# Moving loads, casts and transposes in the hand-ordered prologue of a fused linear-attention and MLP kernel

## The chip, the cores and the metric

The kernel runs on one core of one Trainium2 chip. The metric is the device time of one execution in microseconds (us). The time before is 209.86 us, the median of 5 runs that lie between 209.24 and 211.7.

The core's engines are named as the profile names them: PE is TensorE (matrix products and transposes through the PE array, results in PSUM), DVE is VectorE, ACT is ScalarE, POOL is GpSimd, SP is SyncE, which here only issues DMAs. In the timeline each engine works through its own list in order, and waits for other engines through semaphores.

## What is computed

```python
B, H, S, D = 4, 8, 768, 64                       # q, k, v: [B, H, S, D] float32
for b in range(S // 64):                         # blocks of 64 positions
    intra = (qb @ kb.T) * Dmask                  # Dmask[i, j] = lam_h ** (i - j) for i >= j
    out   = intra @ vb + (qb * lam_pow) @ state  # state: D x D per batch and head
    state = lam ** 64 * state + (kb * rev_pow).T @ vb
x  = out.transpose(0, 2, 1, 3).reshape(B, S, 512)
xn = (x - mean) / sqrt(var + 1e-6) * g_ln
y  = x + relu(xn @ w_ch1) @ w_ch2                # w_ch1: 512 x 2048 (W1), w_ch2: 2048 x 512 (W2)
```

## The kernel before

**Tiling.** The 3072 tokens are cut into 12 windows of 256 positions, numbered u = 0 to 11; window u belongs to batch u mod 4 and to part u div 4 of its sequence. So windows 0 to 3 are the first parts of the four batches. (The change's name calls a window a pair, of two 128-token tiles: the second pair is u = 1, the third u = 2, the fourth u = 3.) A window's k, q and v are three loads of 512 KB each (window 0 in halves of 256 KB). W1 and W2 lie in four pieces each, cast to 16 bits on the way in; the trace counts a piece as 512 KB of what is written.

**Attention of a window.** `in_k` and `in_k_one` cast k to bf16 (L215, L231). `in_q` and `in_q_one` scale q by powers of lam (L226 by halves of the heads, HA and HB; L236 by position parity, all heads). `in_v` scales v (L242). For windows 0 to 2 `transpose_pe` turns k and q on PE into a PSUM tile `tp`, which ACT, or DVE if so told, copies into `kqT` (L250, L251); from window 3 on `transpose_dma` has SP issue a DMA transpose instead (L257). `scores` makes the products of q and k for two of the four head pairs (L273) and `mask` masks them on DVE (L283). `kv` makes the new state's products (L307) and `new_state` the decayed sum (L313, L317, L332). `av` applies the masked scores to v (L419) and `inter` adds the state's part (L432). `inter(u, 0)` ends with `reader(u)`, a DVE copy of eight columns called `seen` (L443): the later `inter(u, 1)` writes the same PSUM tile `po`, so on PE it waits for `seen`. `norm` takes mean and variance and makes the centred tile `xc` (for u >= 2 ACT sums at L458 and DVE makes `xc` at L460); `to_xT` transposes `xc` (L493) and ACT copies it (L494) to `xT`.

**MLP of a window.** A `unit` of the first product is 8 matmuls of 128x256 (L530) and one ACT relu (L533). For windows 0 and 1, `m1a.tile`/`m1b.tile` do the first W1 piece one 128-token tile at a time with 16 matmuls (L641, relu L644). `m1s(m1a, c, lo, hi)` takes the units of W1 piece c. The second product of windows 0 and 1 goes in four parts of 4 matmuls per tile (L667), part n with W2 piece n. DVE finishes a tile at L691.

**Order.** `tc.manual_schedule()` leaves every engine's order as written. Only semaphores for data and for the reuse of buffers are added. From L942 on the calls are listed by hand; `units(n)` interleaves the next n steps of the MLP's list `plan` (L1016 to L1025: first the units of `m1b`, then parts 0 to 3 of the second product).

**Loads.** SP issues the loads of k, q and v (L76), POOL those of W1 (L117) and W2 (L120), since they cast. There are three gates. `behind(t)` is a tiny POOL copy (L728) that waits for the load of `t`, and so holds POOL's later instructions back. `open_in(u, True)` writes one element of the k buffer with a POOL memset (L91), which SP's load of that k, and SP's queue behind it, waits for. And a load that POOL issues after a cast on POOL can't be issued before that cast's own input has landed. POOL's order in the prologue before is: `behind` k of window 0, W1 piece 0, k cast of window 0's HB, v of window 0, `behind` k of window 1, W1 pieces 1 and 2, q of window 1, W1 piece 3, W2 piece 0, v of window 1, `behind` W1 piece 2, memset for window 2, `behind` W2 piece 0, W2 pieces 1 and 2, q of window 2, W2 piece 3, v of window 2, memset for window 3.

Of the kernel before, what the change touches and what calls it, by code (L numbers as in the profile page):

```python
# [12 lines left out]
ACT = mybir.ActivationFunctionType  # L13
# [4 lines left out]
def kernel(  # L18
# [97 lines left out]
    def load_w1(c):  # L116
        nc.gpsimd.dma_start(w1[c], moe_w_ch1[:, c * W1C:(c + 1) * W1C].rearrange("(k p) f -> p k f", p=128))  # L117

    def load_w2(c):
        nc.gpsimd.dma_start(w2[c], moe_w_ch2[c * W2K * 128:(c + 1) * W2K * 128, :].rearrange("(k p) d -> p k d", p=128))  # L120
# [90 lines left out]
    def in_k(u, eng, hs=ALL):  # L211
        src = qkv_in[u]["k"][:, hs].rearrange("p (a e) j d -> p a e j d", e=2)
        dst = part(0, st[u]["kq"], hs)
        for j in range(2):
            (eng.copy if eng is nc.scalar else eng.tensor_copy)(dst[:, :, :, j], src[:, :, :, j])  # L215
# [17 lines left out]
    def in_q_one(u, eng, j):  # L233
        src = qkv_in[u]["q"].rearrange("p (a e) j d -> p a e j d", e=2)
        lq = (lam_q[:, :, j] if u < LB else lam_p[:, 0, :]).rearrange("p (a e) -> p a e", e=2)
        eng.tensor_tensor(part(1, st[u]["kq"], ALL)[:, :, :, j], src[:, :, :, j],  # L236
                          lq[:, :, :, None].to_broadcast([128, NP, 2, D]), op=ALU.mult)

    def in_v(u, eng, hs=ALL):
        n = hs.stop - hs.start  # L240
        lv = lam_v[:, hs, :, None] if u < LB else lam_p[:, 1, hs, None, None]
        eng.tensor_tensor(st[u]["vb"][:, hs], qkv_in[u]["v"][:, hs], lv.to_broadcast([128, n, 2, D]), op=ALU.mult)  # L242

    def transpose_pe(u, a, pairs, eng=None):
        s = st[u]
        n = len(pairs)
        tp = mm_tile([128, n, 2, 128], BF16, "tp")
        for i, p in enumerate(pairs):
            for j in range(2):
                nc.tensor.transpose(tp[:, i, j, :], s["kq"][:, a, p, j], ident)  # L250
        (eng.tensor_copy if eng else nc.scalar.copy)(s["kqT"][:, a, pairs[0]:pairs[0] + n], tp)  # L251
# [27 lines left out]
    def mask(u, hf, heads=(0, 1)):  # L279
        s = st[u]  # L280
        kp = keep.rearrange("p a b t -> p a (b t)")
        for e in heads:
            nc.vector.tensor_tensor(s[f"mA{hf}"][:, e], s[f"sc{hf}"][e],  # L283
                                    kp[:, None, :, :].to_broadcast([128, 2, 2, 128]), op=ALU.mult)
# [30 lines left out]
    def state_sum(u, ab):  # L315
        tmp = wk.tile([128, NP, D], F32, tag="Stmp", name="Stmp")
        nc.vector.tensor_tensor(tmp, st[u]["pk"][ab], state[u % B], op=ALU.add)  # L317
        return tmp
# [154 lines left out]
    def keep_x(u, copy):  # L473
        for ab in range(2):
            copy(st[u]["x"][:, ab], st[u]["po"][ab].rearrange("p h d -> p (h d)"))

    def to_xT(u, ab):
        s = st[u]
        t = 2 * u + ab
        g = group_of[t]  # L480
        i = t - groups[g][0]
        if i == 0:
            xT_of[g] = gp.tile([128, KA, GT * 128], BF16, tag="xT", bufs=3, name="xT")
        dst = xT_of[g][:, :, i * 128:(i + 1) * 128]
        if u >= 2 and u not in X_PE:
            nc.sync.dma_start_transpose(dst, s["xc"][:, ab])
        else:
            if u < 2:
                xt = mm_tile([128, KA, 128], BF16, "xt")
            else:  # L490
                xt = ps.tile([128, KA, 128], BF16, tag=f"po{ab}", name="xt")
            for kk in range(KA):
                nc.tensor.transpose(xt[:, kk, :], s["xc"][:, ab, kk * 128:(kk + 1) * 128], ident)  # L493
            nc.scalar.copy(dst, xt)  # L494
# [230 lines left out]
    def behind(tile_ap):  # L725

        seen_p = wk.tile([128, 1], F32, tag="seen_p", name="seen_p")
        nc.gpsimd.tensor_copy(seen_p, tile_ap)  # L728
# [21 lines left out]
    for i in range(2):  # L750
        nc.scalar.activation(lam_p[:, i], lnlam, ACT.Exp, scale=e_p[:, i:i + 1])
    in_q(0, nc.vector, HA)
    behind(qkv_in[0]["k"][:, 0, 0, 0:1])
    load_w1(0)
    in_k(0, nc.gpsimd, HB)
    in_q(0, nc.vector, HB)
    transpose_pe(0, 1, (0, 1))
    transpose_pe(0, 0, (2, 3), nc.vector)
# [184 lines left out]
    in_k(1, nc.scalar)  # L943
    norm(0, 0, early=True)
    reader(0)
    behind(qkv_in[1]["k"][:, 0, 0, 0:1])
    load_w1(1)
    load_w1(2)
    in_q_one(1, nc.gpsimd, 0)
    in_q_one(1, nc.gpsimd, 1)  # L950
    load_w1(3)
    load_w2(0)
    in_v(1, nc.gpsimd)
    behind(w1[2][:, 0, 0:1])
    open_in(2, True)
    load_in(2, "k", nc.sync)
    load_in(2, "q", nc.sync)
    load_in(2, "v", nc.sync)
    transpose_pe(1, 0, (0, 1), nc.vector)
    transpose_pe(1, 0, (2, 3), nc.vector)  # L960
    to_xT(0, 0)
    inter(0, 1)
    norm(0, 1, early=True)
    st[0]["tmp"] = state_sum(0, 1)
    m1a.tile(0, 0)
    to_xT(0, 1)
    transpose_pe(1, 1, (0, 1), nc.vector)
    transpose_pe(1, 1, (2, 3))
    m1a.tile(0, 1)
    keep_x(0, nc.vector.tensor_copy)  # L970
    nc.scalar.activation(sqrt_first, eps_t, ACT.Sqrt)
    scores(1, 0)
    scores(1, 1, early=True)
    mask(1, 0)
    mask(1, 1)
    m1s(m1a, 1, 0, 1)
    kv(1, "sc")
    new_state(1, 0, nc.scalar)
    m1s(m1a, 1, 1, 2)
    rstd_of(0)  # L980
    m1s(m1a, 2, 0, 1)
    av(1, (0, 1))
    av(1, (2, 3))
    inter(1, 0)
    norm(1, 0, early=True)
    m1s(m1a, 2, 1, 2)
    inter(1, 1)
    norm(1, 1, early=True)
    st[1]["tmp"] = state_sum(1, 1)
    m1s(m1a, 3, 0, 1)  # L990
    to_xT(1, 0)
    m1s(m1a, 3, 1, 2)
    to_xT(1, 1)
    open_window(2)
    in_k_one(2, nc.vector, 0)
    in_k_one(2, nc.vector, 1)
    m1b.tile(0, 0)
    m1b.tile(0, 1)
    keep_x(1, nc.scalar.copy)
    rstd_of(1)  # L1000
    behind(w2[0][:, 0, 0:1])
    load_w2(1)
    load_w2(2)
    in_q_one(2, nc.gpsimd, 0)
    in_q_one(2, nc.gpsimd, 1)
    load_w2(3)
    in_v(2, nc.gpsimd)
    open_in(3, True)
    load_in(3, "k", nc.sync)
    load_in(3, "q", nc.sync)  # L1010
    load_in(3, "v", nc.sync)
    open_in(4, False)
    load_in(4, "k", nc.sync)
    load_in(4, "q", nc.sync)
    load_in(4, "v", nc.sync)
    plan = [(m1b, n) for n in range(m1b.count // NWC, m1b.count)]  # L1016
    plan += [(m2, i, part) for part in range(KB // 4) for m2, i in ((m2a, 0), (m2a, 1), (m2b, 0))]
    plan += [(m2b, 1, part) for part in range(KB // 4)]
# [10 lines left out]
    def units(n):  # L1029
        for _ in range(n):  # L1030
            f, *a = next(steps)
            f(*a)


    units(1)
    transpose_pe(2, 0, (0, 1, 2, 3))
    units(2)
    transpose_pe(2, 1, (0, 1, 2, 3))
    new_state(0, 1, nc.gpsimd)
    new_state(1, 1, nc.gpsimd)  # L1040
# [1 line left out]
    s1b(2)  # L1042
    units(2)
    s2(2)
    units(2)
    s0(2)
    units(2)
    s3(2)
    units(2)
    s4(2)  # L1050
    open_window(3)
    in_k_one(3, nc.vector, 0)
    in_k_one(3, nc.vector, 1)
# [2 lines left out]
    in_v(3, nc.gpsimd)  # L1056
    transpose_dma(3, 0)
    transpose_dma(3, 1)
    units(2)
    open_in(5, False)  # L1060
    load_in(5, "k", nc.sync)
# [296 lines left out]
```

## Time and profile before

| what | value |
|---|---|
| median of 5 runs | 209.86 us (209.24 to 211.7) |
| the profiled execution's own time | 210.09 us |
| its span, first to last instruction | 208.4 us |
| PE busy in the span | 197.4 us, 95% |
| PE work after 200 us (the tail) | 4.39 us of 8.40 us |

The span is the profiled execution between its first and last instruction; what lies around it is 210.09 - 208.4 = 1.7 us. In a timeline row the first number is the start and the second the length, in us from the span's start; then come engine, line, operation, what it writes and reads, shapes and count, and in brackets the engine's idle time just before and what ended it. Where rows of one kind follow each other they are merged into one.

When each load of the prologue was issued (timeline) and when it landed (issue plus the time to landing of the DMA view):

| load | issued | to landing | landed |
|---|---|---|---|
| k, window 1 | 5.43 | 6.7 | 12.1 |
| W1 piece 0 | 5.70 | 8.8 | 14.5 |
| q, window 1 | 6.22 | 9.6 | 15.8 |
| v, window 1 | 7.97 | not told | |
| W1 piece 1 | 12.32 | 8.3 | 20.6 |
| W1 piece 2 | 13.13 | 10.1 | 23.2 |
| W1 piece 3 | 17.87 | 7.9 | 25.7 |
| W2 piece 0 | 18.67 | 10.0 | 28.7 |
| k, window 2 | 23.55 | 6.5 | 30.1 |
| q, window 2 | 23.96 | 8.1 | 32.1 |
| v, window 2 | 24.59 | 9.0 | 33.6 |
| W2 piece 1 | 29.27 | 7.8 | 37.1 |
| W2 piece 2 | 30.07 | 11.0 | 41.1 |
| W2 piece 3 | 34.14 | 10.4 | 44.5 |
| k, window 3 | 36.95 | 8.7 | 45.6 |
| q, window 3 | 37.41 | 9.7 | 47.1 |
| k, window 5 | 54.38 | 4.7 | 59.1 |

### The profile page before, as it was taken

What the parts mean: (1) busy time and instruction counts of PE and PEld (TensorE: products, weight loads), DVE (VectorE), ACT (ScalarE), POOL (GpSimd) and SP (SyncE); (2) the same over time, 40 slices, a digit from 0 to 9 for tenths busy, and PEclk for the clock granted to TensorE, in tenths of its full rate; (3) what the DMA queues carried; (4) which work ended last, traced back from release to release, by engine and by line L of the source; (5) the groups of instructions that cost most, each with busy time, mean ns of one, the idle gap of its engine ahead of it and who ended that gap; (6) DMA issues with size and microseconds to landing.
All of it is one profiled execution on the core that took longest, in us unless ns stands there. A gap on an engine that the chain in (4) does not pass through costs nothing.

```text
span 208.4 us, 7231 instructions
## 1 busy us (share of the span) xinstructions
PE 197.4 (95%) x3099; PEld 156.2 (75%) x3099; DVE 137.0 (66%) x277; ACT 120.0 (58%) x277; POOL 84.0 (40%) x116
## 2 busy tenths in 40 slices
PE   1988999999999999999999999999999999999992
PEld 0477787554775577478888888888888888888881
DVE  2588570529584877758798775667776857865253
ACT  3865779235245567448566775485596575652630
POOL 4649138319847340627255440871282202002020
PEclk9999999999999999999999999999999999999999
DMA  4999999999999999994897899898968020078403
GB/s 108 298 271 216 209 298 164 192 273 273 186 319 175 218 166 217 210 255 83 182 211 111 181 213 159 204 199 121 227 134 190 6 50 3 16 129 278 139 5 97
DMA packets 91043, 36.39 MB, mean 175 GB/s; under 512 B 65154, under 2 KB 88194, under 8 KB 91011
## 3 DMA queue, kind: packets, MB, share of 16 engines
q1 hardware_dynamic: 86400, 31.53, 72.2%
q0 software_dynamic: 4224, 4.19, 12.7%
q8 instruction: 24, 0.39, 0.8%
q10 hardware_dynamic: 386, 0.20, 0.4%
q14 instruction: 9, 0.07, 0.2%
HBM read 27.27 MB, written 6.29 MB: 161 GB/s over the span
## 4 chain that ended last, share of the span: by engine, by line
PE 76%; DMA 12%; DVE 5%; SPq 2%; POOL 2%; issue 1%; POOLq 0%; ACT 0%; DVEq 0%
PE pm L530 33%; PE pm L667 14%; PE pwd L565 6%; PE pwa L565 6%; PE pwc L565 6%; DMA w<-in_moe_w_ch_dram 5%; DMA qin<-in_q_dram 4%; DMA kin<-in_k_dram 3%; PE pwb L565 3%; SPq L76 2%; PE po L432 1%; PE po L419 1%; DVE x L578 1%; PE sc L273 1%; DVE wt L788 1%; PE po L406 1%
## 5 line engine op out<-in xcount | busy, mean ns | idle before, releaser
L530 PE MATMUL pm<-xT,w 128*128 128x256 bf16 x736 | 84.9, 273 | 0.4 <-DMA w<-in_moe_w_ch_dram 0.3
L530 PEld LDWEIGHTS <-w 128*128 128x128 bf16 x736 | 70.4, 98 | 10.2 <-DMA w<-in_moe_w_ch_dram 0.8
L533 ACT ACTIVATE hT<-pm 128x512 f16<-128x512 f32 x92 | 53.9, 597 | 30.1 <-PE pm L530 30.0
L667 PE MATMUL pm<-w,hT 128*128 128x512 f16 x128 | 30.2, 380 | 0.0
L565 PEld LDWEIGHTS <-hs 128*128 128x128 f16 x256 | 24.9, 98 | 2.9
L590 POOL TENSOR_TENSOR x<-ev_u,x 128x256 f32<-128x256 f32 x8 | 5.8, 725 | 51.3 <-ACT ev_u L589 39.9
L313 POOL TENSOR_TENSOR Sn<-Stmp,lam_s 128x256 bf16<-128x256 f32 x16 | 9.8, 615 | 37.9 <-DVE Stmp L391 18.4
L548 DVE TENSOR_TENSOR hs<-hT 128x1024 f16<-128x1024 f16 x16 | 13.9, 872 | 16.0 <-ACT hT L533 15.9
L667 PEld LDWEIGHTS <-hT 128*128 128x128 f16 x128 | 11.6, 98 | 12.1
L565 PEld LDWEIGHTS <-hT 128*128 128x128 f16 x192 | 18.8, 98 | 2.2
L283 DVE TENSOR_TENSOR mA<-sc,keep 128x512 bf16<-128x512 f32 x20 | 13.1, 683 | 7.1 <-PE sc L273 7.1
L458 ACT ACTIVATE x<-po 128x512 f32<-128x512 f32 x18 | 10.6, 590 | 9.9 <-PE po L419 5.3
L460 DVE SCALAR_TENSOR_TENSOR xc<-po,nmean,g_row 128x512 bf16<-128x512 f32 x18 | 13.0, 746 | 3.7 <-ACT nmean L459 3.6
L236 POOL TENSOR_TENSOR kq<-qin,lam_q 128x512 bf16<-128x512 f32 x10 | 10.4, 1063 | 7.5 <-DMA qin<-in_q_dram 7.5
L503 ACT ACTIVATE sq<-x,nmean 128x512 bf16<-128x512 f32 x18 | 12.9, 719 | 0.3
L242 POOL TENSOR_TENSOR vb<-vin,lam_p 128x1024 bf16<-128x1024 f32 x6 | 11.4, 1896 | 3.0 <-DMA vin<-in_v_dram 2.9
L242 POOL TENSOR_TENSOR vb<-vin,lam_v 128x1024 bf16<-128x1024 f32 (+1 forms) x7 | 11.8, 1688 | 1.1 <-ACT kqT L251 0.9
L494 ACT COPY xT<-xt 128x512 bf16<-128x512 bf16 x10 | 5.8, 582 | 7.7 <-PE xt L493 7.7
L578 DVE SCALAR_TENSOR_TENSOR x<-pwd,rstd,x 128x256 f32<-128x256 f32 x16 | 7.7, 482 | 3.6 <-POOL x L598 3.6
L236 POOL TENSOR_TENSOR kq<-qin,lam_p 128x512 bf16<-128x512 f32 x9 | 9.3, 1042 | 1.9 <-DMA qin<-in_q_dram 1.9
L578 DVE SCALAR_TENSOR_TENSOR x<-pwa,rstd,x 128x512 f32<-128x512 f32 (+1 forms) x16 | 9.1, 612 | 0.8
L565 PE MATMUL pwa<-w,hT 128*128 128x256 f16 x64 | 9.6, 273 | 0.0
(129 smaller groups left out, 298.6 us busy)
## 6 DMA issues: line engine op xcount, KB each, us to landing
out_dram<-x SPq DMA_DIRECT2D x22, 256.0 KB, 3.8
w<-in_moe_w_ch_dram POOLq DMA_DIRECT2D x8, 512.0 KB, 9.4
kin<-in_k_dram SPq DMA_DIRECT2D x14, 256.0 KB, 5.1
qin<-in_q_dram SPq DMA_DIRECT2D x14, 256.0 KB, 4.6
vin<-in_v_dram SPq DMA_DIRECT2D x14, 256.0 KB, 5.1
kin<-in_k_dram SPq DMA_DIRECT2D x5, 512.0 KB, 6.7
qin<-in_q_dram SPq DMA_DIRECT2D x5, 512.0 KB, 8.8
vin<-in_v_dram SPq DMA_DIRECT2D x5, 512.0 KB, 8.4
```

What stands on the lines that cost most here:

```text
L236: eng.tensor_tensor(part(1, st[u]["kq"], ALL)[:, :, :, j], src[:, :, :, j], lq[:, :, :, None].to_broadcast([128, NP, 2, D]), op=ALU.mult)
L242: eng.tensor_tensor(st[u]["vb"][:, hs], qkv_in[u]["v"][:, hs], lv.to_broadcast([128, n, 2, D]), op=ALU.mult)
L283: nc.vector.tensor_tensor(s[f"mA{hf}"][:, e], s[f"sc{hf}"][e], kp[:, None, :, :].to_broadcast([128, 2, 2, 128]), op=ALU.mult)
L458: nc.scalar.activation(x, po, ACT.Copy, accum_out=sm)
L460: nc.vector.scalar_tensor_tensor(xc, in0=po, scalar=nm, in1=g_row, op0=ALU.add, op1=ALU.mult)
L503: nc.scalar.activation(sq, s["x"][:, ab], ACT.Square, bias=s["nmean"][:, ab:ab + 1], accum_out=ss[:, ab:ab + 1])
L530: nc.tensor.matmul(pm[:, b, :], lhsT=w1[n // W2K][:, kk, (n % W2K) * 128:(n % W2K + 1) * 128], rhs=xT_of[g][:, kk, 0:N], start=(b == 0 and ...
L533: nc.scalar.activation(hT[:, u * NB:(u + 1) * NB, 0:N], pm, ACT.Relu)
L548: nc.vector.tensor_tensor(s13, b[:, :, 1:2, :].to_broadcast([128, n, 2, 128]), b[:, :, 0:4:3, :], op=ALU.subtract)
L565: nc.tensor.matmul(pr[bank], lhsT=lhs(r), rhs=rhs, start=(first and r == 0), stop=(r == KB // 2 - 1), skip_group_check=True)
L578: nc.vector.scalar_tensor_tensor(out, in0=in0, scalar=r[ab], in1=in1, op0=ALU.mult, op1=ALU.add)
L667: nc.tensor.matmul(acc[i], lhsT=hT[:, kk, i * 128:(i + 1) * 128], rhs=w2[kk // W2K][:, kk % W2K, :], start=(kk == 0), stop=(kk == KB - 1))
```

## The change

The work is the same: the same matmuls, casts and loads. What moves:

- W1 piece 0 is issued by POOL after the cast of window 0's second half of k, no longer ahead of it behind the landing of the first half. W1 pieces 1, 2 and 3 are each issued behind a cast of window 1: q's HA, q's HB, v.
- W2 pieces 0 and 1 are issued behind the landing of window 2's k, pieces 2 and 3 behind window 2's q casts.
- On PE, window 1's first two q transposes come ahead of the first `m1a` tile, and its scores ahead of the second; the copy of those transposes goes from DVE to ACT, and so does `keep_x(0)`. The table load for the square root, `rstd_of(0)` and `rstd_of(1)` move to after window 2's scores.
- Window 3's casts and DMA transposes move from after window 2's second `inter` and norm to before window 2's `av`. On SP the load of window 4's v comes after those transposes.

```diff
     in_q(0, nc.vector, HA)
-    behind(qkv_in[0]["k"][:, 0, 0, 0:1])
+    in_k(0, nc.gpsimd, HB)
     load_w1(0)
-    in_k(0, nc.gpsimd, HB)
     in_q(0, nc.vector, HB)
...
     reader(0)
-    behind(qkv_in[1]["k"][:, 0, 0, 0:1])
+    in_q(1, nc.gpsimd, HA)
     load_w1(1)
+    in_q(1, nc.gpsimd, HB)
     load_w1(2)
-    in_q_one(1, nc.gpsimd, 0)
-    in_q_one(1, nc.gpsimd, 1)
+    in_v(1, nc.gpsimd)
     load_w1(3)
-    load_w2(0)
-    in_v(1, nc.gpsimd)
     behind(w1[2][:, 0, 0:1])
     open_in(2, True)
     load_in(2, "k", nc.sync)
     load_in(2, "q", nc.sync)
     load_in(2, "v", nc.sync)
+    behind(qkv_in[2]["k"][:, 0, 0, 0:1])
+    load_w2(0)
+    load_w2(1)
     transpose_pe(1, 0, (0, 1), nc.vector)
     transpose_pe(1, 0, (2, 3), nc.vector)
     to_xT(0, 0)
     inter(0, 1)
     norm(0, 1, early=True)
     st[0]["tmp"] = state_sum(0, 1)
+    transpose_pe(1, 1, (0, 1))
     m1a.tile(0, 0)
+    transpose_pe(1, 1, (2, 3))
     to_xT(0, 1)
-    transpose_pe(1, 1, (0, 1), nc.vector)
-    transpose_pe(1, 1, (2, 3))
+    scores(1, 0)
+    mask(1, 0)
+    scores(1, 1, early=True)
+    mask(1, 1)
+    keep_x(0, nc.scalar.copy)
     m1a.tile(0, 1)
-    keep_x(0, nc.vector.tensor_copy)
-    nc.scalar.activation(sqrt_first, eps_t, ACT.Sqrt)
-    scores(1, 0)
-    scores(1, 1, early=True)
-    mask(1, 0)
-    mask(1, 1)
-    m1s(m1a, 1, 0, 1)
     kv(1, "sc")
     new_state(1, 0, nc.scalar)
-    m1s(m1a, 1, 1, 2)
-    rstd_of(0)
-    m1s(m1a, 2, 0, 1)
+    m1s(m1a, 1, 0, 2)
     av(1, (0, 1))
     av(1, (2, 3))
     inter(1, 0)
     norm(1, 0, early=True)
-    m1s(m1a, 2, 1, 2)
+    m1s(m1a, 2, 0, 1)
     inter(1, 1)
     norm(1, 1, early=True)
     st[1]["tmp"] = state_sum(1, 1)
+    m1s(m1a, 2, 1, 2)
+    to_xT(1, 0)
     m1s(m1a, 3, 0, 1)
-    to_xT(1, 0)
+    to_xT(1, 1)
     m1s(m1a, 3, 1, 2)
-    to_xT(1, 1)
     open_window(2)
     in_k_one(2, nc.vector, 0)
     in_k_one(2, nc.vector, 1)
+    in_q_one(2, nc.gpsimd, 0)
+    in_q_one(2, nc.gpsimd, 1)
     m1b.tile(0, 0)
     m1b.tile(0, 1)
     keep_x(1, nc.scalar.copy)
-    rstd_of(1)
-    behind(w2[0][:, 0, 0:1])
-    load_w2(1)
     load_w2(2)
-    in_q_one(2, nc.gpsimd, 0)
-    in_q_one(2, nc.gpsimd, 1)
     load_w2(3)
+    open_in(3, True)
     in_v(2, nc.gpsimd)
-    open_in(3, True)
     load_in(3, "k", nc.sync)
     load_in(3, "q", nc.sync)
     load_in(3, "v", nc.sync)
     open_in(4, False)
     load_in(4, "k", nc.sync)
     load_in(4, "q", nc.sync)
-    load_in(4, "v", nc.sync)
...
-    units(1)
+    units(2)
     transpose_pe(2, 0, (0, 1, 2, 3))
-    units(2)
+    units(1)
     transpose_pe(2, 1, (0, 1, 2, 3))
...
     s2(2)
+    nc.scalar.activation(sqrt_first, eps_t, ACT.Sqrt)
+    rstd_of(0)
+    rstd_of(1)
     units(2)
     s0(2)
-    units(2)
-    s3(2)
-    units(2)
-    s4(2)
     open_window(3)
     in_k_one(3, nc.vector, 0)
     in_k_one(3, nc.vector, 1)
     in_q_one(3, nc.gpsimd, 0)
     in_q_one(3, nc.gpsimd, 1)
     in_v(3, nc.gpsimd)
     transpose_dma(3, 0)
     transpose_dma(3, 1)
+    load_in(4, "v", nc.sync)
+    units(2)
+    s3(2)
+    units(2)
+    s4(2)
     units(2)
```

Here `s1b(2)` and `s2(2)` are window 2's two halves of scores and mask, `s0(2)` its `kv` and states, `s3(2)` is `av(2)`, `inter(2, 0)` and the norm of its first tile, `s4(2)` is `inter(2, 1)` and the norm of its second tile.

More of the change, by code (lines that the diff above doesn't have):

```diff
@@ L1032, in units @@
             f(*a)
+    units(2)
+    transpose_pe(2, 0, (0, 1, 2, 3))
     units(1)
-    transpose_pe(2, 0, (0, 1, 2, 3))
-    units(2)
     transpose_pe(2, 1, (0, 1, 2, 3))
```

## The prediction, on record before the result

> **What bounds the kernel now.** I read the page first (busy shares and slices), then busy time by stretches, then the timelines of PE and DVE, last the DMA views.
>
> The page: PE is busy 95% of the span, and the DMA engines are full from slice 2 to slice 18.
>
> ```profile
> span 208.4 us, 7231 instructions
> PE 197.4 (95%) x3099; PEld 156.2 (75%) x3099; DVE 137.0 (66%) x277; ACT 120.0 (58%) x277; POOL 84.0 (40%) x116
> ...
> DMA  4999999999999999994897899898968020078403
> ```
>
> By stretches (length, PE busy, then the other engines): from 35 us on PE has no slack.
>
> ```profile
> 4.00:16.00 12.00, 10.61 (x177) 6.49 (x178) 7.63 (x22) 8.55 (x22) 5.98 (x10) 1.00 1.16 284
> 16.00:35.00 19.00, 17.93 (x320) 14.96 (x320) 10.68 (x24) 13.90 (x29) 10.20 (x14) 1.00 1.17 227
> 35.00:48.00 13.00, 13.00 (x208) 7.23 (x206) 5.37 (x10) 4.34 (x10) 4.38 (x6) 1.00 1.08 228
> 48.00:200.00 152.00, 151.51 (x2363) 123.82 (x2361) 108.49 (x208) 90.97 (x215) 59.77 (x75) 1.00 0.83 164
> ```
>
> So a delay of PE before 48 us reaches the end whole: only 0.5 us of PE idle is left until 200. A gain can come from PE's waits before 35 us alone, 1.07 us of idle plus slow stretches. PE's timeline there:
>
> ```profile
> 15.91 1.72 PE L641 MATMUL pm1t<-xT,w 128*128 128x128 bf16 x16 [0.32 <-ACT xT L494]
> 17.70 1.01 PE L250 MATMUL tp<-ident,kq 128*128 128x128 bf16 x8
> 18.80 1.05 PE L641 MATMUL pm1t<-xT,w 128*128 128x128 bf16 x16
> 20.70 1.05 PE L530 MATMUL pm<-xT,w 128*128 128x256 bf16 x8 [0.27 <-DMA w<-in_moe_w_ch_dram]
> 34.24 0.56 PE L250 MATMUL tp<-ident,kq 128*128 128x128 bf16 x7 [0.33 <-POOL kq L236]
> 45.66 0.31 PE L432 MATMUL po<-Sn,kqT 64*64 64x64 bf16 x8
> ```
>
> The last row is `inter(2, 1)`, which comes at once, for `seen` (DVE, 43.94) is long done. DVE's timeline around it: k of window 3 is cast behind both `xc` of window 2.
>
> ```profile
> 30.16 0.95 DVE L231 CAST kq<-kin 128x512 bf16<-128x512 f32 x2 [1.28 <-DMA kin<-in_k_dram]
> 43.94 0.17 DVE L443 COPY seen<-po 128x8 f32<-128x8 f32 x1 [1.60 <-PE po L432]
> 46.98 0.75 DVE L460 SCALAR_TENSOR_TENSOR xc<-po,nmean,g_row 128x512 bf16<-128x512 f32 x1 [1.44 <-ACT nmean L459]
> 47.64 2.16 DVE L231 CAST kq<-kin 128x512 bf16<-128x512 f32 x2
> ```
>
> The DMA view of 37 to 40 us. SP issued window 3's k, q and v in this stretch (36.95, 37.41, 38.89), yet only q0, POOL's queue with W2, moved data.
>
> ```profile
> q0 software_dynamic: 501, 0.50, 115.0%
> ...
> kin<-in_k_dram SPq DMA_DIRECT2D x1, 512.0 KB, 8.7
> ```
>
> With the table of landings, every one that is told in the order of issue, whichever queue issued it, this says: a load waits for all that was issued before it. That is the rule I cost the loads by.
>
> **The change part by part.**
>
> 1. *W1 piece 0 later.* It is issued at 8.16 (POOL's k cast, 7.26 + 0.90), no longer 5.70, and so behind window 1's v (7.97). With its own 8.8 to landing: 17.0. Ends: 14.5 as before, if the shorter queue ahead gives the delay back; 18.1 if it takes the last place of its group (piece 1 at 20.6 less one W1 spacing, 25.7 - 23.2 = 2.5). I take 17.0, its own row. The first tile on PE starts at 17.05, not 15.91: 1.1 us late.
>
> 2. *Window 1's q earlier, W1 pieces 1 to 3 behind casts.* q loses piece 0 ahead of it: 15.8 - (14.5 - 12.1) = 13.4. HA's two products on POOL have no row; between 0.90 (two casts of that size, 7.26) and 2.05 (two of twice the size, 15.87), I take half of the latter, 1.05. Piece 1 is issued at 14.5, piece 2 near 16.5, piece 3 behind v's product (1.92) near 19. The DMA engines still have work in hand then, and what must land ahead of pieces 1 to 3 is the same, so they land at 20.6, 23.2 and 25.7 again: 0. If the engines run dry first, up to 1 us.
>
> 3. *PE's new order up to 34 us*, from rows: tile 0 17.05 to 18.05; relu (0.60) to 18.85; `kqT` copy (0.58) to 19.4; `xT` copy to 20.0; tile 1 20.0 to 21.0; `kv` 0.35; units 2 and 3 to 23.2; `av` and `inter` 0.9, to 24.1; unit 4 to 25.05; `inter` 25.3; unit 5 26.25; transpose 26.5; unit 6 27.45; second `xc` (DVE from 24.1: 0.17 and twice 0.69 + 0.18 + 0.75) 27.5, transpose to 27.8; unit 7 28.75; both `m1b` tiles to 30.55. Before: 30.63. The lateness is given back because q's transposes, 1.01 for eight (0.61 at 31.51), the masks behind DVE's `keep_x` (1.28) and the W1 wait (0.27) no longer hold PE. Then the 0.33 wait for window 2's q goes: PE is 0.3 early. Ends: 0.9 early with the tile at 15.91, when the W1 landings hold it; 0.7 late at 18.1. PE's first 16 matmuls of L641 took 1.72, the next 16 took 1.05; should such a slow stretch last through tile 1, add 0.7.
>    The Trainium skill, "TensorE: Matmul & The Clock Gate", Part 1, says that PE runs at half clock until it has been busy for a window of about 3.4 us, which agrees with the 1.72 against 1.05. By it, a wait for W1 that spoils a window would keep PE at half clock for 3.4 us more and cost an estimated 1.7 us; no row here shows that case.
>
> 4. *Window 2's loads ahead of W2.* The gate is the same (piece 2 landed, SP issues at 23.55), but no W2 piece lies ahead. A lone load takes 4.7 (window 5's k): k lands at 28.2, q and v with before's spacings (2.0, 1.5) at 30.2 and 31.7. It is earlier by 1.9 than before, though a W2 piece (3.0) went from ahead of it: between W1's last piece and this k the DMA engines run dry for about 1.1 us (28.2 - 25.7 - 1.4, the k's own spacing before). That time W2 loses. W2 pieces 0 and 1 are issued from 28.8, pieces 2 and 3 behind q's casts (30.4 to 32.45), to 34.1. All lie behind v. With before's spacings 3.0, 3.5, 4.0, 3.4 they land at 34.7, 38.2, 42.2, 45.6, each ahead of its use (37.7, 41.2, 44.8, 47.9): 0 for PE.
>
> 5. *Window 3's k cast ahead of `seen`.* Window 3's k is issued at 34.3, not 36.95, but still behind all of W2: 45.6 + 1.1 = 46.7. DVE now has its cast in front of `seen`, both `xc` and the L691 of window 0. Cast 0.95 (30.16; the 2.16 at 47.64 ran beside POOL's q products, which have not begun), `seen` 0.17, three hand-overs of 0.1: PE's `inter(2, 1)` starts at 48.0, not 45.66. Cost 2.4, and PE's 0.3 goes into it. Ends: W2 at W1's spacing (2.5) puts k at 42.8: no wait, 0.3 gained. W2 at 4.0 and k 1.5 behind put it at 49.2: cost 4.9. I take 46.7, for its spacings are those of the same loads.
>    Behind it: `xc` of the first tile is done by 49.0, of the second (ACT 1.0, DVE 0.75) by 50.7; PE asks for them at 50.3 and 51.8. No second wait.
>    The Trainium skill, "DMA: Bandwidth & Descriptors", "Queues, rings and completion order", says that each DMA engine takes turns between the queues that have work, packet by packet. By it, k, issued at 34.3, would share the engines with W2, land near 42 by an estimate, and this part would cost nothing. The rows of 37 to 40 us show no such sharing.
>
> 6. *SP's queue.* The first DMA transpose now waits for the cast (47.8), the second for POOL's q products (q 48.2, to 50.4), 2.0 to 2.3 of issue each; window 4's v goes from 46.98 to about 52.6, lands near 58, its product on POOL ends near 60. Its user, `kv(4)`, is at 69.70; POOL's next state waited for DVE until 60.27. The transposes land near 56.7 (4.1), needed at 58.0 + 2.4. Hidden; without that cover PE would wait for the difference.
>
> 7. *ACT.* Table load 1.28, first root 0.20, two `std` of 0.33 fall into ACT's idle 5.3 ahead of 43.83; two reciprocals on DVE are done near 41, when the states' products come (41.36). 0; 2.1 if that gap were gone. The `keep_x` copies on ACT (1.07) lie ahead of tile 1's relu, with PSUM buffers in hand: 0.
>
> Sum: +2.4 at `inter(2, 1)`, nothing given back: span 208.4 + 2.4 = 210.8, that execution 210.1 + 2.4 = 212.5; the median lies 0.2 below it: **212.3**.
>
> **The rivals.**
>
> A (0.60): the sum above, k cast as the last to be ready; landing 45.6 to 47.9 gives +1.3 to +3.6, 211.2 to 213.5.
>
> B (0.22), not slower: k lands before 44.4 (45.66 - 1.3) and DVE is done when PE comes. For it: k is issued 2.6 us sooner, and W1's spacing is 2.5 against W2's 3.4 to 4.0. Against it: k landed at 45.6 with the same bytes ahead and DMA engines that never ran dry. Then part 3 decides: 209.6, or 210.6 where PE is 0.7 late.
>
> C (0.12): PE itself comes after 48.0. Needs tile 0 after 19.5, or 18.1 with PE slow for long. Against it: part 1's upper end is 18.1. Some +3.2: 213.1.
>
> D (0.06): part 1 costs nothing and B holds: PE 0.9 early, and at best the 0.5 of idle after 48 us gone too: 208.5.
>
> **How the numbers follow.** A measurement of this kernel can tell about 1%, 2.1 us, from no change; that is 207.8 and 212.0. A lies above 212.0 in six of ten cases (0.37) and C always: slower 0.50. The rest of A, B and most of D are within: 0.45. Faster 0.05: all of PE's waits before 35 us, and the 0.5 later, would have to go. The range leaves out D, the lowest of B and the top of C: 209.4 to 213.9. A's own range is 211.2 to 213.5.
>
> **What would show it.** Right: W1 piece 0 landing near 17 and tile 0 just after; DMA engines idle near 24 to 25; window 2's k near 28.2; W2 piece 3 and then window 3's k near 46; PE idle 2 to 3 us ahead of L432 near 48, with DVE's L231 right behind the landing. Wrong: window 3's k landing before W2 piece 3, or before 44.4; tile 0 at 15.9; PE idle elsewhere.

## The result, and the profile after

The changed kernel takes 211.18 us (median of 32 runs, 209.99 to 216.6); the kernel before, timed beside it, 210.07 us (58 runs, 209.24 to 213.48). The ratio is 1.0052, with a 95% interval of 1.0034 to 1.0070. So it is slower, by about 1.1 us and not by the 2.4 of the forecast. The profiled execution took 210.57 us, its span 208.9: 0.5 us over that of before, while the medians are 1.1 apart. One profile of each kernel is thus not enough here, and the spread from run to run becomes part of the question. Medians and ranges hold all runs, while the ratios leave out those more than 1.5% above the fastest of their kernel (of the changed one 215.77 and 216.6), so a ratio need not be the quotient of two medians.

The page of the changed kernel: the span, the busy shares and the DMA engines' slices.

```profile
span 208.9 us, 7229 instructions
...
PE 197.5 (95%) x3099; PEld 157.0 (75%) x3099; DVE 132.8 (64%) x274; ACT 121.6 (58%) x280; POOL 83.3 (40%) x116
...
DMA  4999999999999999997897999897978020178403
```

Busy time by stretches, changed kernel (columns as before: length, PE, PEld, DVE, ACT, POOL, PE clock, DMA share, GB/s).

```profile
4.00:16.00 12.00, 11.02 (x179) 6.66 (x179) 7.75 (x22) 8.51 (x22) 6.66 (x10) 1.00 1.17 277
16.00:35.00 19.00, 16.92 (x302) 14.84 (x302) 8.65 (x19) 12.29 (x26) 9.50 (x15) 1.00 1.12 207
35.00:48.00 13.00, 13.00 (x214) 7.67 (x212) 5.09 (x12) 7.49 (x17) 3.64 (x5) 1.00 1.19 236
48.00:200.00 152.00, 151.93 (x2369) 123.98 (x2368) 106.27 (x207) 91.08 (x215) 59.88 (x75) 1.00 0.88 166
```

PE works 0.4 us more than before ahead of 16 us (11.02 busy against 10.61) and 1.0 less between 16 and 35 us (16.92 against 17.93); it loses nothing from 35 to 48, where the forecast had its wait, and 0.4 us less than before after 48 (151.93 busy against 151.51). Its timeline, and DVE's, changed kernel:

```profile
17.48 1.89 PE L641 MATMUL pm1t<-xT,w 128*128 128x128 bf16 x16 [1.43 <-DMA w<-in_moe_w_ch_dram]
...
21.08 1.07 PE L641 MATMUL pm1t<-xT,w 128*128 128x128 bf16 x16
...
24.40 0.61 PE L419 MATMUL po<-vb,mA 64*64 64x64 bf16 x52
25.48 0.29 PE L419 MATMUL po<-vb,mA 64*64 64x64 bf16 x12 [0.47 <-issue]
...
46.80 0.31 PE L432 MATMUL po<-Sn,kqT 64*64 64x64 bf16 x8
```

```profile
45.88 0.76 DVE L231 CAST kq<-kin 128x512 bf16<-128x512 f32 x2 [2.41 <-DMA kin<-in_k_dram]
46.56 0.16 DVE L443 COPY seen<-po 128x8 f32<-128x8 f32 x1
...
56.14 0.42 DVE L787 TENSOR_TENSOR wt<-w 128x512 f16<-128x512 f16 x1
```

The first tile comes 1.57 later than before, and `inter(2, 1)` 1.14 later, without a wait: `seen` is done at 46.72 and PE has just arrived. That is the place where the forecast had PE waiting until 48.0. After it, part of the lateness goes: the first rows of L667 behind window 3's masks start at 64.33, against 63.84 before, 0.49 later. The reason is in this pair of rows of before, DVE and then POOL, whose place in the changed kernel is the row of 56.14 above:

```profile
55.01 2.00 DVE L788 TENSOR_TENSOR wt<-w 128x512 f16<-128x512 f16 x1
...
54.83 1.90 POOL L242 TENSOR_TENSOR vb<-vin,lam_v 128x1024 bf16<-128x1024 f32 x1
```

DVE makes sums of W2's pieces there (`wt`, `w_sums`), six operations of 0.42. The first takes 2.00 in before, since POOL's product of window 4's v runs at the same time, and the masks behind the sums come late: PE waits 0.43. In the changed kernel v of window 4 is loaded later, its product runs at 58.49, and no sum meets it. That is close, and luck: the last of the six sums ends at 58.48. In two later runs with the same loads (a_busy and after_again), where PE and DVE were later, a sum took 2.00 and 2.12, and PE waited 0.42 and 0.55. The Trainium skill, "SBUF — State Buffer", "Who interferes with whom", says that a VectorE operation with two SBUF inputs and a GpSimd operation that reads SBUF exclude each other, so the later one stands still until the other ends. This agrees: the sum ends at 57.0, just after the product's 56.73, while masks, which read PSUM, kept their 1.29 for two beside POOL's products.

The DMA view of 39 to 44 us, changed kernel:

```profile
q0 software_dynamic: 705, 0.70, 84.1%
q1 hardware_dynamic: 684, 0.35, 34.4%
```

W2 (q0, POOL's queue) and window 3's k (q1, SP's queue) move at the same time, nearly as many packets of one as of the other. The rule of the forecast, that a load waits for all that was issued before it, fails here.

### The profile page after: what moved, and what is told of

The parts are those of the page before. It is cut to its first block, busy times and chain, and to the rows that moved or that the text cites. A ratio compares the mean times of both kernels' runs of the same rounds, so it can differ in the third digit from the quotient of the medians.

```text
span 208.9 us, 7229 instructions
## 1 busy us (share of the span) xinstructions
PE 197.5 (95%) x3099; PEld 157.0 (75%) x3099; DVE 132.8 (64%) x274; ACT 121.6 (58%) x280; POOL 83.3 (40%) x116
## 4 chain that ended last, share of the span: by engine, by line
PE 85%; DMA 7%; DVE 3%; issue 1%; POOL 1%; SPq 0%; POOLq 0%; ACT 0%; DVEq 0%
PE pm L530 38%; PE pm L667 14%; PE pwd L565 6%; PE pwa L565 6%; PE pwc L565 6%; DMA w<-in_moe_w_ch_dram 5%; PE pwb L565 3%; DMA kin<-in_k_dram 2%; PE pm1t L641 2%; PE po L419 2%; PE po L432 1%; PE sc L273 1%; PE xt L493 1%; DVE x L578 1%; PE po L406 1%; PE pk L307 1%
## 5 line engine op out<-in xcount | busy, mean ns | idle before, releaser
L667 PE MATMUL pm<-w,hT 128*128 128x512 f16 x128 | 30.2, 380 | 0.0
L548 DVE TENSOR_TENSOR hs<-hT 128x1024 f16<-128x1024 f16 x16 | 14.3, 895 | 16.2 <-ACT hT L533 16.2
L667 PEld LDWEIGHTS <-hT 128*128 128x128 f16 x128 | 11.7, 98 | 12.1
L242 POOL TENSOR_TENSOR vb<-vin,lam_p 128x1024 bf16<-128x1024 f32 x6 | 11.4, 1896 | 3.8 <-DMA vin<-in_v_dram 3.8
L236 POOL TENSOR_TENSOR kq<-qin,lam_q 128x512 bf16<-128x512 f32 x8 | 8.2, 1050 | 3.8 <-DMA qin<-in_q_dram 3.8
```

Source lines behind the costliest of these rows:

```text
L548: nc.vector.tensor_tensor(s13, b[:, :, 1:2, :].to_broadcast([128, n, 2, 128]), b[:, :, 0:4:3, :], op=ALU.subtract)
L667: nc.tensor.matmul(acc[i], lhsT=hT[:, kk, i * 128:(i + 1) * 128], rhs=w2[kk // W2K][:, kk % W2K, :], start=(kk == 0), stop=(kk == KB - 1))
```

## The experiments

The theory after the result has three terms. (i) W1 piece 0 comes later, so PE arrives late at `inter(2, 1)`. (ii) Window 3's k is cast ahead of `seen`: PE can't pass before k has landed and about 0.9 has gone by; the landing varies, so this costs nothing in one run and 2 or 3 us in another. (iii) Sums of W2 that meet POOL's products make PE wait near 60 us, 0.42 to 1.83 in all in the traces that have it. The rivals are that one of them carries all, or that the order of PE's work or of the other loads does. In the diffs, "changed" and "before" name the kernel that is edited.

### First four: undoing parts of the change

**a_w1p0_early_tile_first**: changed, with W1 piece 0 issued early again and the first tile ahead of the transposes.

```diff
-    in_k(0, nc.gpsimd, HB)
+    behind(qkv_in[0]["k"][:, 0, 0, 0:1])
     load_w1(0)
+    in_k(0, nc.gpsimd, HB)
...
-    transpose_pe(1, 1, (0, 1))
     m1a.tile(0, 0)
+    transpose_pe(1, 1, (0, 1))
```

> The changed kernel, with W1 piece 0 issued behind the landing of window 0's k again, and window 1's first q transposes behind tile 0 on PE again. W1 theory (piece 0's landing at 17.4 us is the whole cost): tile 0 starts near 15.9, PE's clock is full near 17.4, PE comes to inter(2, 1) at 45.3 to 45.7, and the time falls by 1.1 us against the changed kernel. Cast theory (window 3's k cast ahead of the DVE copy seen sets the time of inter(2, 1)): k of window 3 lands at 45.8 still, PE waits there until 46.8, and the time falls by 0.2 at most. Two limits at the same time (PE's own lateness and the cast both end at 46.8): the same as the cast theory here.

Measured: 216.87 us, ratio 1.0301 (1.0258 to 1.0344). The tile came at 16.51, but piece 0 now lies ahead of window 1's q (landed 15.64, not 13.13). POOL issues W1 pieces 1 to 3 behind that q's casts, so they land at 22.39, 26.36 and 28.91, and all later loads follow. PE's timeline in this run:

```profile
26.41 1.05 PE L530 MATMUL pm<-xT,w 128*128 128x256 bf16 x8 [1.29 <-DMA w<-in_moe_w_ch_dram]
...
50.62 0.31 PE L432 MATMUL po<-Sn,kqT 64*64 64x64 bf16 x8 [3.17 <-DVE seen L443]
50.86 3.04 PE L667 MATMUL pm<-w,hT 128*128 128x512 f16 x8
```

So the two edits of POOL's order belong together: with W1 pieces behind casts, piece 0 must be behind q. And here term (ii) is seen whole: 3.17 of wait. After it 8 matmuls of L667 take 3.04 instead of 1.90; the granted clock was at half from 51.47 to 54.88.

**a_cast3_late**: changed, with window 3's casts and transposes behind `s4(2)` and window 4's v load back, as in before.

```diff
     load_in(4, "q", nc.sync)
+    load_in(4, "v", nc.sync)
...
+    units(2)
+    s3(2)
+    units(2)
+    s4(2)
     open_window(3)
...
     transpose_dma(3, 1)
-    load_in(4, "v", nc.sync)
-    units(2)
-    s3(2)
-    units(2)
-    s4(2)
```

> The changed kernel with window 3's casts and DMA transposes back behind window 2's second norm, and window 4's v load back behind its q. W1 theory: inter(2, 1) at 46.8 again; the time is the same, or up to 0.5 us more if the 0.43 wait of PE near 60 us, which went away with the late v load, is back. Cast theory: inter(2, 1) 1.1 earlier than in the changed kernel, time 1.1 less. Two limits: like the W1 theory.

Measured: 211.06, ratio 1.0055 (1.0029 to 1.0080): no gain. `inter(2, 1)` came at 46.30 with no wait, although k landed only at 48.23; but now the sums met POOL's products of q and v of window 4. DVE's timeline:

```profile
55.64 0.82 DVE L787 TENSOR_TENSOR wt<-w 128x512 f16<-128x512 f16 x1
56.38 1.26 DVE L788 TENSOR_TENSOR wt<-w 128x512 f16<-128x512 f16 x1
57.67 2.01 DVE L790 TENSOR_TENSOR wt<-w,wt 128x512 f16<-128x512 f16 x1
```

PE waited 0.92 and 0.71 for the masks. Term (ii) gone, term (iii) in its place, in this execution at least: it took 212.18, the longest of the 12, so it tells of the spread and not of the median.

**a_both_undone**: both edits together.

> The changed kernel with both parts undone: W1 piece 0 early and tile 0 first, window 3's casts late. W1 theory and two limits: inter(2, 1) at 45.3 to 45.7, time 0.7 to 1.1 less than the changed kernel's (1.1, less up to 0.5 for the wait near 60 us). Cast theory: as with the casts undone alone, 1.1 less, and W1's part adds nothing to it. Only under two limits is this run faster than both single undoings.

Measured: 213.68, ratio 1.0159 (1.0123 to 1.0194). W1 pieces late as in the first run (PE waits 0.58), sums of 1.04, 1.26 and 2.01; `inter(2, 1)` at 47.34 with no wait for `seen`. Against the first run this is 3.2 us faster: so much window 3's early cast costs where k lands late (49.13 here), net of the sums' collisions.

**a_busy**: changed, with four more matmuls whose result isn't used, in PE's wait ahead of the first tile.

```diff
     transpose_pe(1, 1, (0, 1))
+    keep_busy(4, "sc")
     m1a.tile(0, 0)
```

> The changed kernel with four idle 128x512 matmuls (extra work, results unused) on PE between window 1's first q transposes and tile 0, in the time in which PE waits for W1 piece 0. If the slow stretch of PE (16 matmuls of L641 in 1.89 us, the full rate only from 20.9) comes from the idle time before it: full rate from near 17.4, tile 0 in about 1.1, PE 0.7 to 1.0 earlier at tile 1, then inter(2, 1) still held by the window 3 cast at 46.8 under the cast and two-limit theories (time the same within 0.2), or 0.7 to 1.0 earlier under the W1 theory. If the stretch has another cause: 17.5 start, 1.9 long, time the same or up to 0.3 more.

Measured: 212.13, ratio 1.0080 (1.0048 to 1.0112). PE's timeline in this run:

```profile
17.59 1.91 PE L641 MATMUL pm1t<-xT,w 128*128 128x128 bf16 x16
...
21.15 1.05 PE L641 MATMUL pm1t<-xT,w 128*128 128x128 bf16 x16
...
48.48 0.31 PE L432 MATMUL po<-Sn,kqT 64*64 64x64 bf16 x8 [2.07 <-DVE seen L443]
```

The clock records of the trace begin at 19.76, with full clock, instead of at 20.93 (ahead of the first record nothing is told of the clock, and the column of the stretches has 1.00 there). That is still behind the first tile, which takes 1.91 again, so this run didn't take the slow stretch away and can't tell what it costs. The second tile comes at 21.15, no sooner than 21.08, since ACT's chain of the relu (19.54 to 20.14), the copy to `kqT` (to 20.61) and the copy to `xT` (to 21.10) starts only when the slow tile has ended. `inter(2, 1)` waited 2.07 for `seen`; k was cast at 47.59.

### Next four: doing one part alone

**b_w1p0_late**: before, with W1 piece 0 behind POOL's cast of k.

```diff
-    behind(qkv_in[0]["k"][:, 0, 0, 0:1])
+    in_k(0, nc.gpsimd, HB)
     load_w1(0)
-    in_k(0, nc.gpsimd, HB)
```

> The kernel before, with W1 piece 0 issued behind the POOL cast of window 0's second half of k, and nothing else. W1 theory: the piece lands near 17.4 and not 14.5, tile 0 starts near 17.5, and since PE has nothing else to do in this order, most of 1.6 us stays: inter(2, 1) 0.6 to 1.4 later than before, time 0.6 to 1.4 more. Rival (PE gives it back behind tile 0, because the W1 pieces behind it and window 1's q set the pace): time within 0.3 of before.

Measured: 211.12, ratio 1.0045 (1.0024 to 1.0067). The tile came at 17.56, `inter(2, 1)` at 47.26; window 1's v landed only at 22.2 and cost PE 0.95 of it.

**b_cast3_early**: before, with window 3's casts and transposes ahead of `s3(2)` and window 4's v load behind them (the reverse of the diff of a_cast3_late).

> The kernel before, with window 3's casts and DMA transposes ahead of window 2's av, and window 4's v load behind them, and nothing else. Cast theory: k of window 3 lands at 45.6 as before, the cast (0.76) and seen behind it, inter(2, 1) starts at 46.6 to 47.0 with an idle time ended by seen on DVE; 1.0 to 1.3 later than before; the wait near 60 us (0.45) goes because POOL's product of v of window 4 comes later: time 0.5 to 0.9 more. If the cast hides (rival): no idle ahead of inter(2, 1), and the time is 0.45 less than before.

Measured: 211.68, ratio 1.0056 (1.0026 to 1.0085). k landed at 45.79 and `seen` was done before PE came at 47.20: no wait in the profiled run, for PE was late by itself (it stood still for 1.31 near 26 us, see the last section). A sum took 2.12.

**b_v4_late**: before, with only window 4's v load behind window 3's transposes.

```diff
     load_in(4, "q", nc.sync)
-    load_in(4, "v", nc.sync)
...
     transpose_dma(3, 1)
+    load_in(4, "v", nc.sync)
```

> The kernel before, with the load of window 4's v behind window 3's DMA transposes on SP, and nothing else. Collision theory: the W sums on DVE (0.42 each, the first one 2.00 while POOL makes the product of window 4's v) keep 0.42 each, because that product starts near 58; PE's wait of 0.43 near 60.8 goes; time 0.4 to 0.5 less than before. Rival: the wait comes from the masks' own place behind six W sums, and stays: time the same. Against both: window 4's v too late for POOL's next state, time more.

Measured: 211.55, ratio 1.0059 (1.0024 to 1.0095): slower, where a gain was expected. The sums met the product all the same (2.12 at 58.06), for PE and DVE were late already. That lateness is the find of this run, since up to 44 us its instructions are those of before, in the same order, and yet `inter(2, 1)` came at 47.13 instead of 45.66. PE's and POOL's timelines:

```profile
24.04 0.45 PE L307 MATMUL pk<-vb,kq 64*64 64x64 bf16 x32 [1.74 <-POOL vb L242]
...
22.09 1.90 POOL L242 TENSOR_TENSOR vb<-vin,lam_v 128x1024 bf16<-128x1024 f32 x1 [2.79 <-DMA vin<-in_v_dram]
```

Window 1's v landed at 22.1. In the profile of before its product starts at 19.42, with no wait. What differs is that window 1's k landed at 11.4, not 12.1, so POOL issued W1 pieces 1 and 2 at 11.70, not 12.32. So before has a race of W1 against v, which costs PE 1 to 2 us when it is lost. The other traces with these loads agree: v late with the pieces issued at 11.74 and 11.82, just in time at 11.80, in time at 12.32, 13.20 and 13.66, and at 14.7 in the last two kernels, which gate them. So the moment of issue isn't all of it: at 11.80 v's product started at 19.80, at 11.82 it started at 21.13. Why so small a difference of issue moves v by 1 to 3 us is not shown. In the changed kernel those pieces are behind q's casts (14.3 and later) and v was in time in all of its traces.

**after_again**: the changed kernel once more, one execution with a profile.

> The changed kernel once more, for a second profile. If the landing of window 3's k decides (cast theory): wherever it lands, inter(2, 1) starts 1.0 behind the landing or when PE comes (46.3 to 46.8), whichever is later; with a landing between 45.8 and 48.2, as the runs so far had it, span 208.9 to 211.5. W1 theory: inter(2, 1) at 46.3 to 46.8 whatever the landing, span 208.5 to 209.2.

Measured: 215.2. Window 1's q landed at 14.95 (13.13 in the first profile), all W1 pieces, W2 and k of window 3 (49.52) behind it; PE's timeline, then DVE's:

```profile
50.44 0.31 PE L432 MATMUL po<-Sn,kqT 64*64 64x64 bf16 x8 [2.91 <-DVE seen L443]
...
49.55 0.76 DVE L231 CAST kq<-kin 128x512 bf16<-128x512 f32 x2 [5.42 <-DMA kin<-in_k_dram]
```

This is the forecast's wait, with its place and its mechanism, and larger than forecast.

### Third four: taking the waits away

**c_k3_first**: changed, with window 3's k gated and issued ahead of W2.

```diff
     behind(qkv_in[2]["k"][:, 0, 0, 0:1])
+    open_in(3, True)
+    load_in(3, "k", nc.sync)
     load_w2(0)
...
-    open_in(3, True)
+    nc.gpsimd.memset(qkv_in[3]["q"][:, 0, 0:1], 0.0)
     in_v(2, nc.gpsimd)
-    load_in(3, "k", nc.sync)
```

> The changed kernel, but window 3's k is gated and issued behind window 2's k and ahead of all of W2 (its q and v stay behind W2, held by a memset of their own). k lands near 34 instead of 45.8 to 49.5 and W2 some 1.4 later each (36.7, 40, 43, 47, uses at 38.9, 42.4, 46.0, 49.1). Theory of three terms: the wait of the second inter of window 2 for the k cast is gone in every run, and what stays is the late W1 piece 0 (+0.5 to +1.1): 210.6, ratio 1.002 to 1.005, and no run near 215. Rival, the k cast never cost anything in the typical run: 211.2 as the changed kernel, with the same spread. Rival, W2 was short of time: PE waits for W2 piece 3 and the time rises to 212 or more.

Measured: 211.27 (210.22 to 211.87), ratio 1.0062 (1.0042 to 1.0082). k landed at 34.53, W2 piece 3 at 48.64. DVE's timeline, then PE's:

```profile
43.64 1.17 DVE L231 CAST kq<-kin 128x512 bf16<-128x512 f32 x2
45.33 0.17 DVE L443 COPY seen<-po 128x8 f32<-128x8 f32 x1 [0.51 <-PE po L432]
...
47.05 0.31 PE L432 MATMUL po<-Sn,kqT 64*64 64x64 bf16 x8
```

The wait is gone, no run of the 12 is above 211.87 (10 of the 32 of the changed kernel are), and the median stays. The other two kernels with the changed issue of W1 and without this wait, a_cast3_late and d_w1_late_waits_gone below, have none above 212.18 either. With the waits of 1.27 to 2.91 in the traces this says that the early cast makes the tail; by itself it doesn't carry the median.

**c_v4_product_later**: changed, with POOL's product of window 4's v behind its state product.

```diff
     in_q_one(4, nc.gpsimd, 1)
-    in_v(4, nc.gpsimd)
...
+    in_v(4, nc.gpsimd)
     open_window(5)
```

> The changed kernel, but POOL's product of window 4's v stands behind POOL's state product of window 3 (60.8 in the trace of the changed kernel), so that POOL is idle while DVE makes the sums of W2 near 56 to 60 us, however late PE is. Theory of three terms: no sum takes 2.0 any more, PE's 0.43 to 0.92 wait near 62 for DVE's masks is gone in all runs; the median falls by 0.2 to 0.6, to 210.7 (ratio 1.001 to 1.004). Rival, the collision is too rare or is given back later: 211.2, ratio 1.005. Rival, the later v products of windows 4 and 5 hold PE near 70 us: 212.

Measured: 211.04, ratio 1.0043 (1.0022 to 1.0064). None of the six sums near 56 to 60 us is above 0.43 and PE doesn't wait near 62. A later sum, at 68.00, now takes 1.26 beside POOL's product of window 5's v, without a wait of PE. But in the profiled run `inter(2, 1)` waited 1.27 for `seen`.

**c_before_v4_product_later**: the same edit in before.

> The kernel before, with the same one move of POOL's product of window 4's v. Theory of three terms: the first sum of W2, 2.00 in the trace of before beside that product, takes 0.42, PE's 0.43 wait near 61 us is gone; 209.6, ratio 0.996 to 0.999, a version faster than both kernels by a little. Rival, the 0.43 is given back later: 210.1, ratio 1.000.

Measured: 211.01 (209.46 to 212.37), ratio 1.0048 (1.0020 to 1.0076). The profiled run is as expected, 210.01 with those six sums at 0.42 or 0.43, but the median is not, and the spread of nearly 3 us agrees with the race of v (pieces 1 and 2 issued at 11.80 here, v just in time). That the race makes this median is argued, not shown.

**before_again**: before against itself.

> The kernel before once more, unchanged, timed against itself: what the comparison can tell. Ratio 1.000 with an interval of about 0.003 each way. A second profile of its prologue: theory of a lucky or unlucky order of landings around 12 us has m1b's first tile on PE at 28.9 in runs near 209.8 and at 30.9 in runs near 211.5; the rival, that the later tile in three other kernels with the same prologue came from their changes, has it at 28.9 again.

Measured: 210.34, ratio 1.0013 (0.9986 to 1.0040). `inter(2, 1)` came at 45.99, and a sum took 2.12 (PE waited 0.71). A ratio of one of these kernels is thus known to about 0.003.

### Last four: what carries the rest

**d_w1_late_waits_gone**: changed, with the edits of c_k3_first and c_v4_product_later together.

> The changed kernel with both later waits taken away: window 3's k issued ahead of W2, and POOL's product of window 4's v behind its state product. W1 piece 0 stays late, as the change has it. Theory (late arrival of PE carries the median, the other two only its spread): 210.9 to 211.2, ratio 1.004 to 1.006, narrow; second inter of window 2 near 46.9 with no wait, no W2 sum over 0.5. Rival (the k cast and the sums carry the median): 210.2, ratio 1.002 or less.

Measured: 210.56, ratio 1.0027 (1.0005 to 1.0048). `inter(2, 1)` at 46.93, no wait, the six sums near 56 to 60 us at 0.41 to 0.43.

**d_w1_as_before_waits_gone**: the same, with W1 issued as in before.

```diff
+    behind(qkv_in[0]["k"][:, 0, 0, 0:1])
+    load_w1(0)
     in_k(0, nc.gpsimd, HB)
-    load_w1(0)
...
-    in_q(1, nc.gpsimd, HA)
+    behind(qkv_in[1]["k"][:, 0, 0, 0:1])
     load_w1(1)
-    in_q(1, nc.gpsimd, HB)
     load_w1(2)
-    in_v(1, nc.gpsimd)
+    in_q(1, nc.gpsimd, HA)
+    in_q(1, nc.gpsimd, HB)
     load_w1(3)
+    in_v(1, nc.gpsimd)
...
-    transpose_pe(1, 1, (0, 1))
     m1a.tile(0, 0)
+    transpose_pe(1, 1, (0, 1))
```

> The same kernel, but W1's pieces issued where the kernel before has them: piece 0 behind the first half of k, pieces 1 and 2 behind k of window 1, piece 3 behind the q products; the first tile comes ahead of window 1's q transposes again. PE's order after that, window 2's loads and the two waits taken away are as in the run beside it. Theory (late arrival): tile 0 near 15.9, second inter of window 2 near 45.9, ratio 0.998 to 1.002, 0.9 us below the run beside it. Rival (the order of PE's work or of window 2's loads is what costs): within 0.3 us of the run beside it.

Measured: 211.27 (210.15 to 213.92), ratio 1.0045 (1.0020 to 1.0071): not faster than the run beside it, against the theory. PE's timeline says why:

```profile
15.90 1.86 PE L641 MATMUL pm1t<-xT,w 128*128 128x128 bf16 x16 [0.32 <-ACT xT L494]
...
23.07 0.45 PE L307 MATMUL pk<-vb,kq 64*64 64x64 bf16 x32 [2.11 <-POOL vb L242]
```

The tile is early, and PE waits for window 1's v instead: the race again, pieces 1 and 2 issued at 11.82.

**e_w1_gated_waits_gone**: that kernel, with W1 pieces 1 and 2 behind the landing of piece 0.

```diff
-    behind(qkv_in[1]["k"][:, 0, 0, 0:1])
+    behind(w1[0][:, 0, 0:1])
     load_w1(1)
```

> The run before last's kernel with W1 issued as in the kernel before and both later waits gone, but W1 pieces 1 and 2 behind the landing of W1 piece 0 (14.5) instead of behind window 1's k (11.4 to 13.0). Theory of the race (W1 pieces 1 and 2 issued before about 11.8 delay window 1's v from 18 or 19 to 21 or 22, and PE waits 2.1 for its product): v lands before 19.5 in every run, PE's wait ahead of L307 is gone, tile 0 stays at 15.9, second inter of window 2 near 46.0; 210.1, ratio 0.999 to 1.003 against 1.0045 without the gate. Rival (late v is no more than a draw that other waits cover): 211.2 as before.

Measured: 210.38 (209.71 to 213.63), ratio 1.0017 (0.9993 to 1.0042). PE's timeline, then POOL's:

```profile
15.86 1.87 PE L641 MATMUL pm1t<-xT,w 128*128 128x128 bf16 x16 [0.32 <-ACT xT L494]
...
45.66 0.31 PE L432 MATMUL po<-Sn,kqT 64*64 64x64 bf16 x8
...
19.41 1.92 POOL L242 TENSOR_TENSOR vb<-vin,lam_v 128x1024 bf16<-128x1024 f32 x1
```

v is in time, `inter(2, 1)` is back at 45.66, the time of before. The profiled execution took 209.81.

**e_before_w1_gated**: before, with the same gate and POOL's product of window 4's v moved.

> The kernel before, with the same gate of W1 pieces 1 and 2 behind the landing of W1 piece 0 and with POOL's product of window 4's v behind its state product. Theory of the race and of the sums: v in time in every run, no W2 sum over 0.6; 209.4 to 209.7, ratio 0.996 to 0.999 and a narrower spread than the 209.46 to 212.37 of the kernel without the gate. Rival: W1 piece 1 now lands later than PE asks for it (20.4) and PE waits some 0.5 more: 210.2 to 210.6.

Measured: 210.31 (209.96 to 210.69), ratio 1.0012 (0.9992 to 1.0031): the narrowest spread of all, and not faster than before; the rival's case. PE waited 0.37 for W1 piece 1 (landed 21.19) and 0.63 for window 2's q.

**What follows.** The ratios form a chain: changed 1.0052; both later waits gone 1.0027; W1 early and v in time as well 1.0017, which can't be told from before against itself, 1.0013. From end to end this is 0.0035, 0.7 us, and by the two intervals it is known to some 0.003 (an estimate that takes them as independent): with the three terms taken away together, the change's cost is gone as far as can be told. The same follows from the last two kernels, which were timed beside the same runs of before and have the same gate of W1 and the same place of window 4's product: 1.0017 with the changed order of PE's work and of window 2's loads, 1.0012 with the order of before. So the rival that this order carries the cost has nothing that could be measured. How the cost divides among the three terms is not shown, for each step of the chain, 0.0025 and 0.0010, is smaller than the 0.003 to which a ratio is known. That neither wait alone, taken away, lowered the time measurably (1.0062 and 1.0043) stays unexplained beyond that. Nor did a kernel come out faster than before.

## Why the prediction was wrong, by its steps

The direction and the range held; the time, 212.3, was 1.1 too high. The step that failed is 5: its +2.4 stands in the sum as a wait of one size, which PE meets early, and step 3, which has PE 0.3 early, was wrong by 1.4. In the profile after the result PE waited 0 at `inter(2, 1)` and came 1.14 late by itself; in three other traces it waited there 1.27 to 2.91.

1. *W1 piece 0 later*: right. Issued 7.99 (8.16 forecast), landed 17.43 (17.0), tile at 17.48 (17.05).
2. *W1 behind casts*: q landed at 13.13 (13.4). Pieces 1 to 3 landed at 20.91, 23.65 and 27.22 (20.6, 23.2, 25.7); the third is late, behind v's product at 18.48, but PE didn't wait for it in the first profile. After a late q, as in after_again, PE waited 0.53 for piece 2.
3. *PE's new order*: wrong by 1.4. PE was to be 0.3 early at `inter(2, 1)` (the step's own 30.63 - 30.55 and 0.33 make 0.4) and was 1.14 late. The working let tile 1 start at 20.0; it started at 21.08. Of this 0.4 is the later start of tile 0, and most of the rest is that the working gave tile 0 1.0, though its row of before has 1.72 for it: it took 1.89, and ACT's three operations behind it ended at 20.96. And PE stood still for 0.47 inside the 64 matmuls of L419, which no row of before showed. As to the clock gate of the Trainium skill ("TensorE: Matmul & The Clock Gate", Part 1), the clock records begin, with full clock, at 20.93 instead of 17.35, so tile 0 lies wholly ahead of the first record of full clock. What a faster tile 0 would be worth in the end no run shows, for it took 1.91 in a_busy too. After the wait of 3.17 in the first experiment the clock was at half for 3.41 us, which agrees with the page's window of about 3.4 us.
4. *Window 2's loads ahead of W2*: right within 0.9: k 29.04 (28.2), q 30.75 (30.2), W2 at 35.26, 38.72, 41.70 and 45.44 (34.7, 38.2, 42.2, 45.6), no wait of PE.
5. *Window 3's k cast ahead of `seen`*: the mechanism is right, the size is not one number. The forecast's landing of 46.7 was 45.8 in the first profile and 46.6 to 49.5 in three others of kernels with the same loads; the wait was 0, 1.27 (c_v4_product_later), 2.07 (a_busy) and 2.91 (after_again). From the cast's start to `inter(2, 1)` went 0.89 in each of these three, where the sum had 1.3 (and its own terms, 0.95 + 0.17 + 0.3, make 1.4). PE's own lateness of 1.1 lies inside the same wait and not beside it: whichever is later counts. Against before, `inter(2, 1)` came 1.14, 1.86, 2.82 and 4.78 later in these four traces, so the forecast's 2.34 lies among them; the changed kernel's median, 211.18, lies between the times of the first two (210.57 and 211.55). The page "DMA: Bandwidth & Descriptors" of the Trainium skill ("Queues, rings and completion order") agrees from 39 us on (705 packets against 684); before k's packets began to move, near 38.5, the queue of W2 was alone, as in before, and k landed 3.8 behind the 42 that the prediction had estimated from the page. So neither rule by itself gives the landing.
6. *SP's queue*: hidden, as said. But "hidden" missed a gain of the first profile: the later v of window 4 moved POOL's product just away from the sums. "Nothing given back" was wrong by 0.65 in the first profile (1.14 late at 46.8, 0.49 at 64.3).
7. *ACT*: right; no wait of PE for the roots, and DVE's reciprocals ran at 41.48.

Of the rivals, B (k in time, PE itself decides) is nearest to the first profile, with PE 1.1 late instead of 0.7, and A to the other three. A's price counted a full wait where PE was late anyway.

## What to carry to other kernels

Where two things must be ready, add no lateness to a wait: work out both times and take the later, for each order in which the loads may land. In a prologue that fills the DMA engines, look at two or three profiles before a step of 1 us is put down to an edit, and time the kernel against itself: here the same instructions came to the same place 1.5 us apart. And a load that is moved moves its cast or product on POOL as well; look at which DVE operations with two SBUF inputs, and which casts, will then run beside it.

## What the runs showed of the hardware

- A DVE operation of 0.42 with two SBUF inputs took 2.00 to 2.12 beside POOL's products, in nine of the traces; the cast at L231, 0.75 for two, took 2.16 in before and 3.30 in e_before_w1_gated beside POOL's products of q and v.
- PE stood still inside one block of equal matmuls (L419, near 25 us), with no wait for any engine: 0.24 to 0.84 in five traces of kernels with the changed order, behind the 52nd matmul, and 0.31 and 1.31 in two with the order of before, behind the 43rd. About the stop of 1.31 the DMA engines were full, and a queue that the DMA view names "instruction" moved one packet of 16 KB, from 24.43 to 25.41, just ahead of the stop (25.38 to 26.70). Every trace has such a packet between 22 and 26 us, and in all seven with a stop PE went on 1.29 to 1.55 behind its end. So the stop ends at a near fixed time behind this packet; that PE waited for instructions which it brought is likely, and not shown, for no run moved the packet by itself.

```profile
24.85 0.54 PE L419 MATMUL po<-vb,mA 64*64 64x64 bf16 x43
26.70 0.35 PE L419 MATMUL po<-vb,mA 64*64 64x64 bf16 x21 [1.31 <-issue]
```

(PE's timeline of b_cast3_early.)
